# Two row fetches on two queues, a bias table behind one of them, six fills for eight and a new order: an attention and expert kernel

## The chip, the cores and the metric

The kernel runs on one core of a Trainium2 chip. The metric is device microseconds of one execution, the median of three runs. Engines are named as the profile names them: PE (TensorE matmuls), PEld (its weight loads), DVE (VectorE), ACT (ScalarE), POOL (GpSimd), SP (SyncE, which issues most DMAs). SPq and ACTq are the instruction streams of SP and ACT where they issue a DMA.

## What is computed

Eight batches, eight heads, 576 positions, head size 64, all float32. First, attention with a causal window of 128 positions and a bias that falls with distance; its result x is then read by four experts, each a full causal attention with its own projections, mixed by the two best of four gate values.

```python
scores = scale * np.matmul(q, k.transpose(0, 1, 3, 2))
bias = slopes[:, None, None] * (-np.abs(rel))[None, :, :]
mask = (rel >= 0) & (rel < window)
scores = np.where(mask, scores + bias[None], -1000000000.0)
attn = np.exp(scores - scores.max(-1)); attn /= attn.sum(-1) + 1e-09
x = np.matmul(attn, v)                      # heads side by side: (8, 576, 512)
logits = x @ w_gate                         # the best 2 of 4 experts, softmax over the two
for e in range(E):
    q, k, v = x @ wq[e], x @ wk[e], x @ wv[e]
    a = softmax(scale * q @ k.T, causal)
    out += weight_of(e) * (a @ v @ wo[e])
```

## The kernel before

Two heads are handled together as a "pair"; there are 32 pairs g, four to a batch. A pair's scores are taken in blocks of 128 rows; each block is added to a bias table and reduced to its row maximum by one DVE instruction (CUSTOM_DVE_ANT_0, called ISA in the program's order), raised by ACT, scaled by POOL or ACT, transposed on PE, and multiplied with v on PE. PSUM holds eight 128x512 tiles (ps0 to ps7).

The first batch's pairs are started in two halves so that work can begin on little data. For the first half, `fetch(g, 1, 0)` brings the rows of the first two blocks of pair g with two DMAs, one for each head (64 partitions of 2x256 floats, 128 KB). All eight go to tiles w100 (pairs 0 and 1) and w101 (pairs 2 and 3). `half_s` and `first_blocks` make the products, and use the table FT (it lies in the tile KKm) that DVE and POOL make out of the bias table tbt, which comes by a DMA of 160 KB. idt is the identity for the transposes. Then the projection weights are loaded: `wload(c)` brings one chunk of 386 KB (in_wall; there are four), `wprep(c)` rounds it to its high part WH (on POOL or ACT) and takes the low part WL (on DVE or POOL). The projections of x multiply chunk by chunk: the tile wx0 of x goes with the first chunk, wx3 with the fourth.

Ahead of all PE work stand "fills" (`warm`, lines 396 to 400): products of a zeroed tile AHTm, 128x512, which nobody reads.

The order of the work is not that in which the code stands. All instructions are recorded into a list (`_Rec`), and `plan` (line 201) puts them out in the order of the table ORDER, which also picks, where `nc.any` gave two choices, the engine. A negative place in ORDER is a fill:

```python
d = lo + 256 * hi
at += (d >> 1) ^ -(d & 1)
if at < 0:
    out.append(alt["fill"])
    continue
i = nodes[at // 2]
out.append(alt.get(i, [ops[i]])[at % 2])
```

Since one place issues everything, nearly every row of the trace has line 1229; rows are told apart by tiles and times. The change touches `fetch` (line 347), the three lines at the head of the emission (`zero()`, the table, the identity) and ORDER.

Of the kernel before, what the change touches and what calls it, by code (L numbers as in the profile page):

```python
# [19 lines left out]
B, H, S, D = 8, 8, 576, 64  # L20
DM = H * D
E = 4
P = 128
# [20 lines left out]
    "b3juEI|B5+l{K*2T#ZFbxq3n=;IMtT1a~MMI_4YiV8m{UccbBmBvWv#s!d9)?n)2tO!(<Xr&i>sj5MF2L(7KhM4D!Hq&5aY0TREpagutw@WEF^80x0A}N_"
    "AIHdMnGX{dei8<A6ll0RKi1?}n@TiOVuipfA+q^!e|Ifi85qxtt084$MOhgpYkrZXYck(5cio-Q3T`u)TGQ|OX5}1<vpV~d<tR&Hh+{B6r@13Pt!q=s&q>"
    "QGEHPJ(52Y8om+eXfvzy2$AN(f3(Jg>e*tT03SnP6m3mrRN3CUYnj$c*^vyw8&f^GP6G9;zy%NfS)7cx?m59=iOmE;_V8qalrvvjzvH7+^)Lb#=<xF9X-$"
    "v1xTwQv6=Y(!g4&LKKn3NeXU*)db<2<9bH;MkO{1ZOnGn!fwe^>00uw6V3i2a(p8Ew;K-qTWXFue1W+%2w;D>tF}A>tP9?ep`4v14edwQ$S%8V5N?|)yj1"
    "5l{CEbzkUhy1~C(xRVHO6ul};=Q&M8X#bMGVg@0o)S!rl)fbSGP*1w9kF3rQj<%P?kJPL7+JXb+N?cmb&@I%8%oLQaTYKKE}R@XtwrEVE9?xZH?gne)$k|"
    "nUJa=>*})<AU}VFR|=wA3;6k^A0n#SmVEe&~+aKiE$mXr=qt*lgMJ-)^<orv_uEXgIJ{#Td*Vhd+5P*#UL!p4K+Zfu|ZGrwD6>iI@MjcMzZ=5fYMz24R4V"
    "Fu85!x&dHpsWf$cYeUPzLWX-5Qrs{L1~?rntDe0$O8}-m@BZanZJqD|8WzbSq7y#)I_n7jP_Jx#;d`u$5qB2`ALuB^vyVJZl6wFF*!#2ZGc0H@(RiD3?W("  # L50
    "iSjvRs15ZUh8*xKF;V@1|lR&EKUE$u6d9X(C}-1ZDaCC0I>>dIv6+T=#0;$oMsghgK8q3hxKG%qAJAvz>6-)YOaxwsPHN!y|}m|3cXh=t4D<@UU}13$D^7"
    "OTpuFp`y<m+yIY`d81Ug(JSOE(>6!wmRHY;IcjO&EqMU9u9?iXn>`(abA6nIO&z4KYXiNQsDX8*rn@|2wAQ7OT-Io1urkJ!EEPMSckWM0PWBL?H=d^=(x}"
    "UVcoy>&<D4wE4*WL(`&;}%rP=0AMe86o39gj&0AI4-NUBxdiCW!8l0XtjsF+J=iVk3<(QG98^kK}7`6}g4T7oJO~_HF*`xHd6p~H|=~lK=TEE%)%IcD`(K"
    "8fpYP5G*yE-m7X;dN|*nvHT?gH$vZPFZ{kUU}CX;hk6trL_5tg0!}d%@FawjJ+!h8VGWdPdu+_kz^+Ww*i_EzXhNitapsd|XZrWJ69mq-CZhTT_;uGw~%h"
    "mvg3jLnaJblxEVRm{Rbz)cIO`Z-o0Q-ZwSAytWKIw;UTgZ@*zTSr@#YqO$3!NB?7FjwmL@M8TOdFx_JrY-%WnK|-$o<ICY$F7H2lwDy)-hNrkX+r(xPWbU"
    "w4H8e}PPrl+L%dkZg=*<g?`>W#2yvO*k;tG26TA4|vAIc#=Vwp%@cyBB$z&x)v4l{tnwdDjXgR4l7gl#}n<j!+Ht63jWm`!1_oIqr&$xck;m*y@i!^)Tp7"
    "Pg*c6!WA<hk+`{t(TX8S_;})TQXx%kJ>>gtAsKKSs5frg{C@I4kc6$sY1d@YU0_iw1z~+#8)#GpGe0`;*wWx!eJlZf(QS4`T;fpYs!)1s*5S?ZqLn*J}N2"
    "6IN7R-8fG!9yOnz4_5ltu#}7&zp%8-4xFZkBbGjzm;B@c{e~yyYUl~P5BcRsMhsf=S^Ca~TJ@-t(K-Rsa^>J{){&?4Z2Evl-0zfYRAU%oitP<aLTJz#B4D"
    "+~5jy?YO8tTG|>=t`t&HUVAoN~Mo@<$)}(Sv36=_xEVA=$+4eJEjo(oLd}%Idnt8oEYkh+=oVMHatHl4i(*zk1>cbBLYiY@dDl&w+M#hK>xkySrEmbauCP"
    "beTPafMhyA6IedU%I?l>Z96{9>+Hr5MCMs(qo=j#u(GArvDOW!yj*=CF%DB0<@<KjT4Apq9;;9;Py_PBAat6B`vw_n_b`()v#MGXRTP%8YbG#v%X63J)Sn"  # L60
    "u?(GNa$l{S3oq0X|JAGiGisw$3G8yalR%ZZ<5zkzqi+v!nPe$JlA&8j2UxH6)Z$Z@lYI%G8rT^Z_ajw=V6-ObT416LO<@d-DS<!Si-bGG+CWM9gxrAh}`o"
    "vCk$U3J}pa;L2=LY=mG|K#Rw{k=~p^-X=#v+VV^jv^N?Nv}z+;H66pX!1acwPxf>U&A7V-2B+HiI+MSyC4c#^%6t^M2#Tg?sNU8!rEFhsiIW^5JqBw?<xt"
    "|R6gdjNH3N5s?nLd0BsS&(#NXfy}KY+5v3R!*OculIyY8qw!QIbj|D<)2Ah?!)5K*V*h{J$R)}r<%x_oQLUU#(sw-xjNgFg~+RK#56H*T#Gq*zJTSxUB%`"
    "@}kX1EAV<-?B9?aAbr9>raobR$y(O+_hWC|j$Ubu1#b0*%iQ@~FGh3A3|!v2UJTfyFsA2_<@V5U8hUkk&g-03DIzFhu&%bo1Ku2Y*uj@ROep2I<j<<*y?@"
    "_Kt%41gZ1*u=B)##l+<UED&eO86cq_{9-Bm7x@{a?jDD(^zF7B9^@1rS{3{7K>v)rwZawA#4=KEA$czJ`erRdYd8ku#WV1#_t_Of9FZ(a&QnU6Y(8?7S^x"
    "RvRk{WnYvxM1<HGmfwJARjdmuaO*3^sleCNN5Z$j04UvFP8$w`E3FrK<=_VnxkWE`gMZKs(cl@w-<mg5qmAn)VvbgqRZOTP)#LW5vZxYD7@x$;v<T&9^Uc"
    "x~e^-_w5CvbA0XVOJO|Uh%>lc(3sLm#yG#3~!(lgHUg=4|+RFEt6i8HQW(ylI4{#*jgiGevMP&)zv2CSC{ky*ba>kiz>54KnP0g&B80M2FraYmD$}TSAPr"
    "ShbL*tJW5*z(h)#gM*g7E<LMbk$Hi<`TF`OQ9qM&vubkGnGC*EANuFL^wpL7zymK$q)^!y(efr&@QQ=Ko++|!{DD+-DaEw-r(?JVgt>HuxGdliR+|T{&N7"
    "-M+y`k(cuRZ^APZe|^UQch(7=TCqqTLx}rdb)h4e<GgL9`1{bkbjrmTEZ;EeqW2T8_bN4Iwe2wK;-<RcLK~@Nd5GFa0C0eQteod2ODeP^~7Wk?BIY1d1#2"
    "Wz%<!i>dvDDTrwK?LW@SFPa#dBxGzC8c5_UWYZQ_S!b(d)}~5_r_nvR%uE(#CrR#|j%l%U4ik0?<BezoilO?R2dp4-+dHC=&pt(yhels|tbEYbJ-!~hI-Z"  # L70
    "@*(%95OZDLpNB+OmHyQX1kW{Q=bbfCd+cK`6#d8uixN8B&{bw*Ywss8q0DKSS<TL&Eqr`B}bAV3Q$@80$v)Iss*pWH(ybO1MaEUf9I`Wmo;<Ba17Xh6keg"
# [1245 lines left out]
```

## Time and profile before

| what | value |
|---|---|
| median of three runs | 462.22 us (461.86 to 462.54) |
| the profiled execution, its own time | 461.31 us |
| its span | 459.5 us |
| PE busy | 452.8 us, 99% |
| PEld busy | 400.3 us, 87% |
| DVE busy | 386.3 us, 84% |
| ACT busy | 367.6 us, 80% |
| POOL busy | 246.8 us, 54% |
| share of PE in the chain that ended last | 87% |

Busy shares are averages over the whole span. Matmuls are pipelined, so that their records overlap: a busy PE can still have short holes. The page's forty slices show PE at nine tenths in all but the first and the last. What the change touches by name lies in the first 25 us; the order is other everywhere.

### The profile page before, as it was taken

The page shows a single profiled execution, that of the slowest core. Times are in us where ns is not written, and L with a number is a line of the kernel's source. Part 1 is how long each engine was busy: PE and PEld are TensorE (multiplying, and loading weights), DVE is VectorE, ACT ScalarE, POOL GpSimd, SP SyncE. Part 2 cuts the span into 40 slices and gives each one's busy share as a digit, 9 for nine tenths or more (in the row PEclk, how much of TensorE's full clock was granted, in tenths as well). Part 3 has the DMA queues.
Part 4 walks back from the last instruction along what each step waited for, and adds up shares of the span by engine and source line. Part 5 has one row for each costly group of instructions (what it writes and reads, how often), then busy time and mean ns, then how long its engine had stood idle before and what let it go on. Part 6 is the DMA issues. An engine that isn't in the chain of part 4 may idle for free.

```text
span 459.5 us, 18916 instructions
## 1 busy us (share of the span) xinstructions
PE 452.8 (99%) x7100; PEld 400.3 (87%) x7100; DVE 386.3 (84%) x1801; ACT 367.6 (80%) x1393; POOL 246.8 (54%) x498
## 2 busy tenths in 40 slices
...
GB/s 191 271 213 156 219 115 61 33 62 132 88 3 208 9 66 99 85 208 28 97 162 81 3 120 190 88 4 10 140 193 104 58 4 3 150 3 1 3 116 116
DMA packets 28252, 44.76 MB, mean 97 GB/s; under 512 B 7680, under 2 KB 14208, under 8 KB 28160
## 3 DMA queue, kind: packets, MB, share of 16 engines
...
q8 instruction: 56, 0.92, 0.8%
...
q14 instruction: 36, 0.29, 0.2%
...
## 4 chain that ended last, share of the span: by engine, by line
PE 87%; DVE 5%; ACT 2%; DMA 2%; POOL 2%; issue 1%; SPq 0%; POOLq 0%; ACTq 0%; DVEq 0%
PE ps L1229 87%; DVE w L1229 2%; ACT w L1229 2%; POOL w L1229 1%; DMA w<-in_rd 1%; DVE ps L1229 1%; DMA w<-in_wall 1%; DVE WL L1229 1%; DVE MPL L1229 0%; ACT MPL L1229 0%; DVE r L1229 0%; POOL MPL L1229 0%; DVE wx L1229 0%; DVE mr L1229 0%; POOL wx L1229 0%
## 5 line engine op out<-in xcount | busy, mean ns | idle before, releaser
L1229 ACT COPY w<-ps 128x512 f32<-128x512 f32 (+4 forms) x252 | 99.5, 445 | 33.7 <-PE ps L1229 29.2
L1229 ACT ACTIVATE w<-w,nm 128x128 f32<-128x128 f32 x252 | 98.7, 395 | 13.0 <-DVE nm L1229 12.7
L1229 PE MATMUL ps<-wx,WH 128*128 128x288 f32 (+2 forms) x512 | 107.5, 299 | 0.0
L1229 POOL TENSOR_SCALAR w<-w,mr,w 128x128 f32<-128x128 f32 (+3 forms) x128 | 79.8, 635 | 29.4 <-DVE mr L1229 16.7
L1229 POOL TENSOR_SCALAR w<-w,r 128x128 f32<-128x128 f32 (+1 forms) x163 | 60.9, 387 | 52.6 <-DVE r L1229 14.8
L1229 PEld LDWEIGHTS ps<-wx,WH 128*128 128x128 f32 x512 | 82.0, 189 | 2.4 <-DVE mnm L1229 0.7
L1229 ACT ACTIVATE w<-w,mnm 128x512 f32<-128x512 f32 (+3 forms) x128 | 71.2, 561 | 5.2 <-DVE mnm L1229 4.9
L1229 DVE TENSOR_TENSOR w<-ps,tmt 128x768 f32<-128x768 f32 (+2 forms) x92 | 69.8, 775 | 5.4 <-PE ps L1229 5.0
L1229 DVE CUSTOM_DVE_ANT_0 w<-ps,tbt 128x128 f32<-128x128 f32 x272 | 68.7, 284 | 0.9 <-PE ps L1229 0.2
L1229 PE MATMUL ps<-wx,WL 128*128 128x288 f32 (+2 forms) x256 | 68.5, 296 | 0.0
L1229 PE MATMUL ps<-w 64*64 64x128 f32 (+4 forms) x1200 | 63.5, 309 | 0.1
L1229 PE MATMUL ps<-WH,wx 128*128 128x260 f32 x288 | 61.4, 288 | 0.9 <-ACT WH L1229 0.9
L1229 PE MATMUL ps<-w,vt 64*64 64x192 f32 (+4 forms) x1344 | 59.7, 282 | 0.0
L1229 PE MATMUL ps<-idt,w 64*128 64x64 f32 (+1 forms) x1160 | 58.4, 230 | 1.0 <-POOL w L1229 0.9
L1229 PEld LDWEIGHTS ps<-w 64*64 64x64 f32 (+1 forms) x1200 | 50.2, 135 | 8.4 <-issue 1.4
L1229 PEld LDWEIGHTS ps<-w,vt 64*64 64x64 f32 (+1 forms) x1344 | 52.4, 133 | 5.2 <-issue 1.9
L1229 PEld LDWEIGHTS ps<-idt,w 64*128 64x128 f32 (+1 forms) x1160 | 47.7, 139 | 7.8 <-issue 2.0
L1229 DVE COPY_PREDICATED ps<-mkt,ps 128x64 f32<-128x64 int32 (+2 forms) x184 | 53.3, 313 | 1.2 <-PE ps L1229 0.5
L1229 PE MATMUL ps<-w,w 64*64 64x64 f32 (+7 forms) x1088 | 52.5, 307 | 0.0
L1229 DVE COPY w<-ps 128x256 f32<-128x256 f32 (+5 forms) x94 | 42.4, 469 | 11.8 <-PE ps L1229 11.1
L1229 PE MATMUL ps<-KKm 64*64 64x288 f32 (+8 forms) x640 | 50.5, 410 | 0.0
L1229 ACT ACTIVATE w<-w,r 128x128 f32<-128x128 f32 (+1 forms) x125 | 45.0, 398 | 6.2 <-DVE r L1229 3.9
...
## 6 DMA issues: line engine op xcount, KB each, us to landing
...
w<-in_hd SPq DMA_DIRECT2D x14, 128.0 KB, 3.3
w<-in_wall SPq DMA_DIRECT2D x4, 386.0 KB, 5.5
out<-w SPq DMA_DIRECT2D x8, 128.0 KB, 2.4
...
```

The lines of the kernel that those rows point to most:

```text
L1229: getattr(getattr(tc.nc, e), m)(*a, **k)
```

## The change

The two row fetches of pairs 0 and 1 get a choice of queue (SP or ACT), and so do the bias table and the identity. ORDER is replaced: the new one has six negative places for eight, puts one fetch of pair 0 on ACT ahead of the table, the identity on SP, and has another order of all engines. The recorded steps are the same; with the new table 309 of the steps that have a choice go to the other engine, and in the sums over the program PE differs by the two fills alone.

```diff
 ORDER = (
-    "c-pOae^g{=dH>w|K6Bp}?lm)JrkRN|DOgCM2U;-j6)IFPpb!TO2`DsRAVP%}6bx9fV8AfCRA`t82^=AX1PoMAsE{sZX@}!(52Rq>8!)Vabg|HYUHr0^HDF"
+    "c-p0S4NxT4b#C{)XZl{YTRSb!NHg(_i?N0n9B{yf5=bC{1!YiX95w<8Vvr$*XYhjr9FP|op4k_0AO;5%P(WfLa6pDKM6hBdu)%@^94N6aD1ieun=A?I>?Y"
...
@@ -344,7 +344,11 @@
             for j in range(2):
                 o = D * j * row + (QW + S + 2 * P) * j
                 src = bass.AP(tensor=a.tensor, offset=a.offset + o, ap=[[row, D], [QW - P * j, 2], [1, n]])
-                nc.sync.dma_start(v2[D * j : D * j + D, z, :, :n], src)
+                row_fetch = (v2[D * j : D * j + D, z, :, :n], src)
+                if g < 2:
+                    nc.any(*[(e, "dma_start", row_fetch, {}) for e in ("sync", "scalar")])
+                else:
+                    nc.sync.dma_start(*row_fetch)
             return
...
     zero()
-    nc.scalar.dma_start(tbt[:, 3], tb[:, 3])
+    nc.any(*[(e, "dma_start", (tbt[:, 3], tb[:, 3]), {}) for e in ("scalar", "sync")])
     for g in range(4):
         fetch(g, 1, 0)
-    nc.scalar.dma_start(idt, ident)
+    nc.any(*[(e, "dma_start", (idt, ident), {}) for e in ("scalar", "sync")])
```

What the table does is seen in the order of each engine. First place: the heads of the queues of SP and ACT. Before, SP:

```order
L1229 DMA w100_91<-in_hd 64x2x256 x4
L1229 DMA w101_92<-in_hd 64x2x256 x4
L1229 DMA w100_91<-in_rd 128x2x320
L1229 DMA w100_91<-in_hd 64x2x256 x2
L1229 DMA vt0_125<-in_vd 128x256
```

and ACT:

```order
L1229 DMA tbt_107<-in_tb 128x640
L1229 DMA idt_105<-in_ident 128x128
L1229 ACT_TABLE_LOAD
L1229 ACTIVATE w50_82,sm0_115<-w50_82,nmA0_129 128x128 x2
L1229 ACTIVATE w50_82,sm0_115<-w50_82,nmA0_129 128x256 x2
```

With the change, SP:

```order
L1233 DMA w100_91<-in_hd 64x2x256 x3
L1233 DMA idt_105<-in_ident 128x128
L1233 DMA w101_92<-in_hd 64x2x256 x4
L1233 DMA w100_91<-in_hd 64x2x256
L1233 DMA w100_91<-in_rd 128x2x320
L1233 DMA w100_91<-in_hd 64x2x256
```

and ACT:

```order
L1233 DMA w100_91<-in_hd 64x2x256
L1233 DMA tbt_107<-in_tb 128x640
L1233 ACT_TABLE_LOAD
L1233 ACTIVATE w50_82,sm0_115<-w50_82,nmA0_129 128x256
L1233 ACTIVATE w50_82,sm0_115<-w50_82,nmA0_129 128x128 x2
```

One of the four fetches into w100 went to the head of ACT, the table stands behind it, and the identity stands fourth on SP. Further down SP's queue the four weight chunks stand behind 16, 22, 25 and 27 DMAs, where before it was 14, 17, 20 and 24.

Second place: PE around the first products with the fourth weight chunk (those that read wx3). Before:

```order
L1229 MATMUL ps1_70<-WH_111,wx1_78 128x260 x2
L1229 MATMUL ps1_70<-WH_111,wx2_79 128x260 x2
L1229 MATMUL ps1_70<-WH_111,wx3_80 128x260 x2
L1229 MATMUL ps1_70<-WL_112,wx0_77 128x260
L1229 MATMUL ps1_70<-WL_112,wx1_78 128x260
L1229 MATMUL ps4_73<-wx3_80,WH_111 128x256 x2
L1229 MATMUL ps7_76<-w101_92 128x192
```

With the change:

```order
L1233 MATMUL ps7_76<-wx1_78,WH_111 128x256
L1233 MATMUL ps6_75<-WH_111,wx1_78 128x260
L1233 MATMUL ps7_76<-wx1_78,WH_111 128x256
L1233 MATMUL ps3_72<-wx1_78,WH_111 128x256
L1233 MATMUL ps3_72<-wx3_80,WH_111 128x256
L1233 MATMUL ps5_74<-idt_105,w54_86 128x128
L1233 MATMUL ps3_72<-wx3_80,WH_111 128x256
```

Ahead of the first wx3 product stand 24 products of the other three chunks' high parts before and 30 with the change, and the two 128x192 products of w101, which stood behind it before.

Third place: DVE in the softmax blocks of pairs 5 (nm5) and 6 (nm6); the TENSOR_TENSOR rows with tmt split transposed blocks of pair 4. Before:

```order
L1229 ISA w50_82,nm5_155<-ps6_75,tbt_107 128x128
L1229 ISA nm5_155 128x1
L1229 COPY_PREDICATED ps7_76<-mkt_106,ps7_76 128x128
L1229 TENSOR_TENSOR wx3_80<-ps2_71,wx3_80 128x256
L1229 ISA w51_83,nm6_161<-ps7_76,tbt_107 128x128
L1229 ISA nm6_161 128x1
L1229 ISA w51_83,nm6_161<-ps7_76,tbt_107 128x128
L1229 ISA nm6_161 128x1
L1229 TENSOR_TENSOR w102_93<-ps3_72,tmt_108 128x6x2x64
```

With the change:

```order
L1233 TENSOR_TENSOR w100_91<-ps4_73,tmt_108 128x6x2x64
L1233 ISA w50_82,nm6_161<-ps7_76,tbt_107 128x128
L1233 ISA nm6_161 128x1
L1233 COPY lg0_143<-ps0_69 128x4
L1233 TENSOR_TENSOR w100_91<-ps3_72,tmt_108 128x6x2x64
L1233 ISA w56_88,nm5_155<-ps5_74,tbt_107 128x128
L1233 ISA nm5_155 128x1
```

Two splits of 128x768 (6x2x64) of pair 4 now stand ahead of the last two blocks of pair 5; before, the first of them came behind pair 5's last block.

## Rows read from the trace of the kernel before

**Rows 1.** The page: heading and first section.

```profile
span 459.5 us, 18916 instructions
PE 452.8 (99%) x7100; PEld 400.3 (87%) x7100; DVE 386.3 (84%) x1801; ACT 367.6 (80%) x1393; POOL 246.8 (54%) x498
```

**Rows 2.** Busy time by stretch: engines, PEclk, DMA share, GB/s.

```profile
2.00:4.00 2.00, 2.00 (x6) 1.52 (x6) 0.93 (x2) 0.92 (x1) 0.85 (x2) 1.00 0.93 247
10.00:15.00 5.00, 4.74 (x59) 3.35 (x57) 4.93 (x28) 4.91 (x21) 3.28 (x10) 1.00 0.94 269
15.00:20.00 5.00, 5.00 (x47) 4.12 (x46) 4.97 (x26) 4.49 (x20) 3.79 (x9) 1.00 1.03 281
20.00:25.00 5.00, 4.08 (x50) 3.37 (x49) 4.93 (x17) 2.90 (x13) 4.19 (x6) 1.00 1.07 246
25.00:30.00 5.00, 5.00 (x42) 4.90 (x41) 4.96 (x26) 5.00 (x24) 3.55 (x7) 1.00 0.87 192
40.00:60.00 20.00, 20.00 (x338) 18.30 (x331) 19.41 (x113) 17.30 (x80) 8.45 (x23) 1.00 0.70 175
```

**Rows 3.** Waits of PEld, whole span: us, times, longest.

```profile
PEld ps L1229 <- ACT w L1229: 4.9, 18, 0.5
PEld ps L1229 <- DVE w L1229: 2.8, 10, 0.5
```

**Rows 4.** The timeline's first 7 us: start, us, engine, tiles, idle before.

```profile
0.74 5.34 SPq L1229 DMA_DIRECT2D w<-in_hd  x8
1.10 3.78 PE L1229 MATMUL ps<-AHTm 128*128 128x512 f32 x8 [1.10 <-POOL AHTm L1229]
3.03 0.29 DVE L1229 TENSOR_SCALAR KKm<-tbt 128x256 f32<-128x256 bf16 x1 [3.03 <-DMA tbt<-in_tb]
3.36 0.82 DVE L1229 TENSOR_TENSOR KKm<-KKm,tbt 128x256 f32<-128x256 f32 x1
4.13 0.40 DVE L1229 TENSOR_SCALAR mkt<-tbt 128x128 int32<-128x128 bf16 x1
4.81 4.42 PE L1229 MATMUL ps<-w 64*64 64x128 f32 x64
5.80 0.29 DVE L1229 CUSTOM_DVE_ANT_0 w<-ps,KKm 128x128 f32<-128x128 f32 x1 [1.23 <-PE ps L1229]
6.40 0.29 DVE L1229 CUSTOM_DVE_ANT_0 w<-ps,KKm 128x128 f32<-128x128 f32 x1 [0.30 <-PE ps L1229]
6.62 0.42 DVE L1229 CUSTOM_DVE_ANT_0 w<-ps,KKm 128x256 f32<-128x256 f32 x1
6.96 0.42 DVE L1229 CUSTOM_DVE_ANT_0 w<-ps,KKm 128x256 f32<-128x256 f32 x1
```

**Rows 5.** DMA issues by stretch: KB each, us to landing; first 1.2 us, then 14.3:17.

```profile
tbt<-in_tb ACTq DMA_DIRECT2D x1, 160.0 KB, 2.3
w<-in_hd SPq DMA_DIRECT2D x1, 128.0 KB, 3.4
idt<-in_ident ACTq DMA_DIRECT2D x1, 64.0 KB, 3.2
...
w<-in_wall SPq DMA_DIRECT2D x1, 386.0 KB, 6.9
```

**Rows 6.** The timeline around the projection weights, 14 to 25 us.

```profile
14.99 0.82 PE L1229 MATMUL ps<-w 128*128 128x192 f32 x4
15.49 1.35 SPq L1229 DMA_DIRECT2D w<-in_wall  x1
18.83 1.82 PE L1229 MATMUL ps<-wx,WH 128*128 128x256 f32 x14
22.88 0.74 PE L1229 MATMUL ps<-WH,wx 128*128 128x260 f32 x4
24.10 0.91 ACT L1229 CAST WH<-w 128x260 fp32r<-128x260 f32 x2
24.54 0.51 PE L1229 MATMUL ps<-WH,wx 128*128 128x260 f32 x2 [0.92 <-ACT WH L1229]
```

**Rows 7.** DVE groups by shape, 35 to 60 us.

```profile
L1229 DVE TENSOR_TENSOR w<-ps,tmt 128x768 f32<-128x768 f32 x4 | 3.8, 944 | 0.0
```

**Rows 8.** PE groups by shape: 4.9 to 6.1 us, then 6.6 to 9.2 us.

```profile
L1229 PE MATMUL ps<-w 64*64 64x256 f32 x4 | 1.1, 631 | 0.0
...
L1229 PE MATMUL ps<-w 64*64 64x256 f32 x28 | 2.4, 387 | 0.0
```

More of the change, by code (lines that the diff above doesn't have):

```diff
@@ L44 @@
[L44 to L71, printed above, removed]
@@ new lines @@
+    "4D!Vq^+ep*h9RT12>5C^&ItX*UW3UC|((gpY<@8#jzw>L0L$Sh6GnAMu(YXL4wur{~S;dk1JK29ClTX46eQW3cuIB<Flaz*i4&*fmQ{lVc`JUsePZhR6U&"
+    "BaK-!dB?)>AW5>tNZwT@P!pS_ktp8(_A!be&*K!CnARSCiJ-z744~6+nijt?Y)aWSQcnh7RZi&ul!-waqNA0c1fcNz6DnR$}%*dOO7dH>PHj3KDzcQ&Mk6"
+    "gPlzkP63kAz0oJ_3W2astd^(d__QV5-BK+Ijskwg3S^{ZzcD2|s;lF_ztY#-(w<#`U6X^kFbKH>%%#dc&c@U_yik}2#aWP@T{`YdzmRt&z87o&ElD^c@*}"
+    "F{_2i7AqqL=sQqq+|m7=t9Y$rrksluknk=^+gS5HQXleTtEoD8|VeCF0BpwXinsT~&p%>2z=hMGI<{~>=`iSLiORG+0}V_yPf|KguEr{J*{$g_X^l|PJ&W"
@@ new lines @@
+    "-T{X0V0T+lV4KVld!r!Ww*$+m1&i@6Pmmi5~<JAPpPbeY<5Kv`E(5mYRo4)t2fH|*iEef)R9*R1;zcJR=yEWwq4#6mqWpJW?3j*tp=!B%X{VZOYkuXSF~f"
+    "T&pgbrKkZuGfSNvL+?JN+%q?~I7PQ@}5q|Wrl~|}sFsa5R0BWIXQwuCWv2~xe!)tFe!O#A6Yci>>2BO@_x1RdK*3RWWj~gGEzgb%~cze5liI3c?fJIR)sz"
+    "P#=oZ%YldSViQJE|CppqPC<ctnQH3U4V7^$&gXnbhHKyG8m`+7t}n-Wlm!{S5_Ec~`dn`76|^w6!+bTn-AOSr9%DS<_kTfGgq9fs>jjJo25_!!jV!LFEg0"
+    "5vqoCG{8-OiiE)t4X9g_a0NV2u?4VQnY9kE3`<u5!^+xJdBuD0Os_uwiGJMPH`LZidaRw&n{C;BmO}wLd+Y=!n3eEfeIz0>A=PP(PJlPV6!I#Hap652TUn"
@@ new lines @@
+    "KBi;jb&cr{7}$LzSnnxk%ev%S4g18`-wDX)}dZ){(ys`RqOQ2T_%yI!r3zC$^6zm$d_rKS<j`o6M9ylS3hdf-oAqeA+PJ~MGy-gq<pG$qyva$NY9r!epQ?"
+    "?w&GE%HrOR7<b<B4heGV3S^g&NgU=arS!TZ_KokG0n>)e;3#JY|f-%!wPi4p7$ls)5#f7p}&w&Hyg#h1)JAkTWiq3#(-&Nq4}Bl8fK^2$Y1{AHl`H+@N2a"
+    "kypzo^l@J4vn+?z=eG4++1QzHbkf|%9GO?3+>8G-jm>IqKWP+{KLYbW*kKD#X9mn{jeDkh_%2t~~t)yq5Z-7AqM=Uj6ss{^ml{%P0%=OJz_dJb+Y~&Tnu?"
+    "}lWY+_v%&`Qe)zLtL5TXk}PZ*MAO>*a6c)RWG{6mS!@xOa1741fPmq^G3E8#Cr;)iI$;IW?#BE7VM;2SN5Z``i16>dc<~;!H>R4FDFa+2CUw&bXs5H(6!O"
@@ new lines @@
+    "e%@54WHM@joZ@sACw1WPe)6S_g2sVeH+EUDRetn$NpJt|2#KZrYd{!z$xxbJmg#NWSHmxOhTnd&oiQ8qcCm0DjNdu^QA#F#0f_4)zoA9_=HCMgg~i<n0Gp"
+    "-o`Cs<HNHkH%&K$wfDmEvK=Y9XYd{tQ*`bkg5e~_=7UzX*WEBTGkxGXyXuCm~SwG|e`;lNCuZntoE;<#wI8?&{(g_ZhzPcD#tk|kSZ)zWO9V>_}INT#Hty"
+    "<?jy6Gge1g(tA`H|S_cY0I2%Y__gOWG6$*Vj^QSr*jFaE2=A|W~XMW*V|IZNYRu+^82d~EzSdX8uKxOmB%&%DKSNiLwY$2N6j`<^U9_AYi$)1qv>hsv@)K"
+    "(_kHk8h8&ymP0zdX{#?u<{`uoY_SE^Av~Vh$uTZSa$&j{o5fb9c`^pQts}?Rll2X13<&0Wdp`|?`wyks7x(QuS&M;X~4cE1Oeh0-4L^eY3n%-nY39$LxM;"
```

102 lines of the change are left out of this document (57 added, 45 removed).

## The prediction

> **What bounds the kernel now.** The page comes first: PE is busy 99% of the span [rows 1], so that outside its edges only a shorter stream of PE work, or holes too short for that figure, can be worth much. The table of stretches comes second, because the 99% is a mean over stages. There the reader sees the start: in 20 to 25 us PE has 4.08 us of 5, and from 10 us to 60 us DVE is full (4.93 to 4.97 of each 5 us, 19.41 of 20) [rows 2]. The DMA share is 0.93 to 1.07 in those early stretches. So the first 25 us hang on three things at once: DVE's queue, the bytes that must come, and PE's order. The timeline is read third, to see what DVE waited for at its start [rows 4], and around the projection weights, where PE's one long hole stands, 0.92 us before 24.54, released by ACT's rounding of the fourth weight chunk [rows 6]. After 25 us PE is never shown idle for long; a lead that PE has there is a lead at the end, if the body's order is no worse.
>
> The sum is made against the profiled execution: 461.31 us, 1.8 us more than its span. That is 0.9 us under the median of the three runs, 462.22; a difference worked out here is put on the median. Under 0.2%, about 0.92 us, one can't tell this kernel's change from none.
>
> **The change, part by part.**
>
> *Six fills for eight.* Eight take 3.78 us from 1.10, so 0.47 each [rows 4]; six end at 1.10 + 6 x 0.47 = 3.9. They come to nothing by themselves, either way: what covers them is PE's wait for the rows. The first fetch needs 3.4 us from its issue at 0.74 [rows 4, 5], so it lands at 4.1. If the rows came before 3.9, two fills fewer would be worth up to 0.9 us.
>
> *The second row fetch on ACT.* Eight fetches take SP 5.34 us, 0.67 each [rows 4]. On SP the second is issued 0.67 us behind the first and lands at 1.41 + 3.4 = 4.8, which is where the first products start. At the head of ACT both land at about 4.1, and PE can begin 0.7 us earlier. SP saves one fetch (0.67) and gets the identity; the transposes need that only when a block has been scaled, 5 us later, and its landing takes 3.2 us [rows 5], so it costs them nothing.
>
> *The table behind it.* Here the gain is paid back in part. The table was issued at 0.74 and landed 2.3 us later [rows 5]; DVE began on it at 3.03 and had the bias ready at 3.36 + 0.82 = 4.2, long before PE's products, for which it waited 1.23 us [rows 4]. Now its issue waits for ACT's fetch, to 0.74 + 0.67 = 1.41. Lower end: 1.41 + 2.3 = 3.7. Upper end: what followed the table on that queue, the identity, took 3.2 us, so 4.6. In 2 to 4 us the DMA engines are 0.93 busy at 247 GB/s [rows 2], so the 128 KB that now stand ahead cost 0.5 us of transfer: 3.7 + 0.5 = 4.2, which I take. Behind it DVE does the conversion (3.03 to 3.36, 0.33), then the mask (0.40), which the new order puts ahead of the addition, then the addition (0.82) [rows 4]: ready at 4.2 + 1.55 = 5.75, between 5.25 and 6.15.
>
> The Trainium skill ("DMA: Bandwidth & Descriptors", section "Issuing engines are not separate DMA queues") says that DMAs started from different engines run on the same DMA engines and interleave, and that starting them in parallel saves only the issue time. If each queue brought its own bandwidth, the lower end would stand, and the start would gain 0.9 us; by the rule it is nearer the upper end, and the start gains little. The trace shows two queues at work at 0.93 of the engines, which agrees.
>
> What was the start worth before? Four blocks of pair 0 are done at 6.96 + 0.34 = 7.30. Back to back they take 2 x 0.22 + 2 x 0.34 = 1.12 (6.40 to 6.62, 6.62 to 6.96) [rows 4], so DVE stood as if it had begun at 6.18. With the bias at 5.75 it begins 0.43 us earlier, at the ends 0.9 or 0.0. DVE waits now for the table, no longer for PE; POOL, which makes the other pairs' tables from the same bias, starts later than it did, and its scaling of pair 0 gains less. I carry 0.3 us to PE at 24 us.
>
> *PE's order around the fourth weight chunk.* Six more products with the other chunks stand ahead of the first with wx3, and two of 128x192. At 1.82 / 14 = 0.13 and 0.82 / 4 = 0.2 us each [rows 6] that is 0.78 + 0.4 = 1.2 us of work put into a hole of 0.92 us. PE came to the hole at 22.88 + 0.74 = 23.6; now it comes at 23.6 - 0.3 + 1.2 = 24.5. Is the chunk there? It was issued at 15.49 and landed 6.9 us later, 22.4 [rows 5, 6]. It now stands behind 27 DMAs on SP for 24. By place: (15.49 - 0.74) / 24 = 0.61 each, issue at 17.2, landing at 24.1. By bytes, since the engines are full: ahead of it are 128 KB of pair 2 and 3's tail and 32 KB of small ones more, 160 KB at 269 GB/s (10 to 15 us) [rows 2], 0.6 us, so 23.0. The rounding takes POOL about what ACT needed for both parts, 0.91 [rows 6], the first part some 0.6: ready at 23.6 by bytes, 25.0 by place for both parts. I take the bytes, because the DMA share stays near 1. Then PE has no hole; at 24.5 it stands 1.2 us further than it did at 24.54. By place it would be 0.7.
>
> The later second and third chunks (22 and 25 DMAs ahead for 17 and 20) are covered by w101's 64x192 products, which now stand ahead of all weight products. If that cover fails, PE waits there and the 1.2 us shrinks towards 0.4.
>
> *The rest of the order.* PE's work is the same but for the fills. Its waits are drawn anew: those of PEld on ACT and DVE are 4.9 + 2.8 us in 28 [rows 3], 0.28 each. If each changes by its own size, the sum moves by 0.28 x the root of 28, 1.5 us, with no sign. The tail ends in the same steps. I set it at nothing and give it to the range.
>
> Sum: 0.3 + 0.9, **1.2 us less**: 460.1 for the profiled execution, 461.0 for the median.
>
> **The rivals.**
>
> *Nothing is left at the end (462.0).* DVE is full up to 60 us [rows 2]. If DVE, and not PE's hole, limits this stage, only its earlier start counts, 0.43 us less, and PE's lead at 24.5 is spent waiting for blocks; with the table at its upper end not even that. For it: DVE's 4.9 of 5. Against it: PE is shown busy in 25 to 30 us, 5.00 of 5, so that it had other work.
>
> *Slower (463.7): DVE's queue at pair 5.* Two splits of 128x768 for pair 4 now stand ahead of pair 5's last two blocks. Each takes 0.94 us [rows 7], so the blocks come 1.89 us later at about 46 us, and behind them wait ACT's exponents, their scaling and PE's transposes of pair 5. In that stretch DVE has 0.6 us free of 20 [rows 2] and can't make it up. 1.89 less 0.43 is 1.46 slower: 462.22 + 1.46 = 463.7. It decides if PE has less than 1.9 us of other work in its queue ahead of pair 5's transposes. Against it: the splits have to be done anyway, and pair 4's products come sooner.
>
> *TensorE's lower clock lasts longer (462.4).* Products of 64x256 take 631 ns before 6.1 us and 387 ns after 6.6 [rows 8]; fills come every 0.47 us. The first is the 1.2 GHz level, the second 2.4, although the granted clock reads 1.00 throughout. Now PE stops between the fills' end, 3.9, and 4.1, or longer if the rows are late, and the rise may come later. If it came after 9.2 us, the products of 6.6 to 9.2, 2.4 us of busy time, would take up to 1.3 us more, of which DVE's own pace hides a part; all of it takes the 1.2 us away. The Trainium skill ("TensorE: Matmul & The Clock Gate", Part 1) says that the clock starts low, that activity releases it, and that idle time brings the low state back, out of step with the kernel's start; no run yet shows a gap's effect here.
>
> That the change does not do what it says is excluded by the order shown above.
>
> **How the numbers follow.** My forecast 0.46; nothing left 0.28; slower by DVE's queue 0.20; the clock 0.06, two thirds of it inside 0.2%. So faster by over 0.2% has 0.46, within 0.2% 0.32, slower 0.22. The time is the likeliest case's, 461.0; its own range is 459.5 to 462.3, by 1.5 us of redrawn waits. For 8 in 10 the range goes from 459.0, two us under the forecast (1.5 us and the table at its lower end), to 463.6, nearly the slower rival's time.
>
> **What would show it.** Right: the first CUSTOM_DVE row near 5.75, waiting on the table or on DVE's own addition, not on PE; the first 64-row product near 4.1; no PE wait on WH near 24 us; PE busy in 20 to 25 us above 4.08. Wrong in the table: DVE's first conversion after 4.6. Wrong in the weights: PE idle with a release by POOL's or ACT's WH, or by in_wall. Wrong in the body: the start is as said, and the lead at 25 us is gone by 60 us with PEld waits on DVE between, or later in another place.

## The result, and the profile after

The changed kernel takes **466.24 us** (466.12 to 466.57, 4 runs) against 462.04 for the kernel before (461.17 to 462.54, 4 runs): a ratio of 1.0094, interval 1.0077 to 1.0112. By that ratio it is 4.3 us slower (4.2 by the medians); the prediction, 461.0 (459.0 to 463.6), had the wrong sign. The two profiled executions, one of each kernel, differ by 4.8 us in their spans, 464.3 against 459.5 [rows 1].

The page of the changed kernel: heading, first section, and the shares of the chain that ended last.

```profile
span 464.3 us, 18919 instructions
...
PE 453.6 (98%) x7098; PEld 400.2 (86%) x7098; DVE 389.0 (84%) x1806; ACT 366.1 (79%) x1392; POOL 243.6 (52%) x494
...
PE 74%; DVE 13%; POOL 7%; ACT 3%; issue 2%; DMA 1%; POOLq 0%; DVEq 0%; ACTq 0%
```

The chain's line of the kernel before:

```profile
PE 87%; DVE 5%; ACT 2%; DMA 2%; POOL 2%; issue 1%; SPq 0%; POOLq 0%; ACTq 0%; DVEq 0%
```

PE's idle time has grown from 6.7 us (459.5 less 452.8 [rows 1]) to 10.7 (464.3 less 453.6): four of these 4.8 us. In the chain PE's share was 87%; it is 74%, and DVE and POOL have 20% where they had 7%. So PE waits more often for these two. The stretches say where it begins (columns as in [rows 2]):

```profile
2.00:4.00 2.00, 2.00 (x5) 1.01 (x4) 0.00 (x0) 1.28 (x1) 0.00 (x0) 1.00 0.81 222
10.00:15.00 5.00, 3.95 (x56) 2.60 (x49) 4.81 (x31) 5.00 (x23) 4.08 (x10) 1.00 0.88 243
20.00:25.00 5.00, 5.00 (x62) 4.43 (x59) 4.85 (x23) 5.00 (x24) 4.59 (x9) 1.00 0.96 238
25.00:30.00 5.00, 3.69 (x31) 3.48 (x31) 4.72 (x22) 2.69 (x12) 2.95 (x6) 1.00 0.58 171
40.00:60.00 20.00, 20.00 (x306) 18.78 (x306) 19.48 (x109) 18.09 (x84) 6.93 (x23) 1.00 0.88 210
```

DVE, which worked 0.93 us in 2 to 4 us, does nothing there now. PE's hole of 20 to 25 us is gone, as predicted (5.00 for 4.08), and one of 1.3 us stands in 25 to 30, where PE had been full. In 10 to 15 us PE has 3.95 for 4.74; from 40 to 60 us it is full in both. The timeline of the first 9 us, to set beside [rows 4]:

```profile
1.10 2.93 PE L1233 MATMUL ps<-AHTm 128*128 128x512 f32 x6 [1.10 <-POOL AHTm L1233]
1.50 0.61 ACTq L1233 DMA_DIRECT2D tbt<-in_tb  x1
...
4.60 1.55 PE L1233 MATMUL ps<-w 64*64 64x256 f32 x12 [0.58 <-DMA w<-in_hd]
5.04 0.29 DVE L1233 TENSOR_SCALAR KKm<-tbt 128x256 f32<-128x256 bf16 x1 [4.07 <-DMA tbt<-in_tb]
...
5.59 0.41 DVE L1233 TENSOR_TENSOR KKm<-KKm,tbt 128x256 f32<-128x256 f32 x1
...
6.18 0.42 DVE L1233 CUSTOM_DVE_ANT_0 w<-ps,KKm 128x256 f32<-128x256 f32 x1 [0.18 <-PE ps L1233]
...
6.67 3.26 PE L1233 MATMUL ps<-w 64*64 64x128 f32 x38 [0.52 <-DVE nmA L1233]
...
8.80 0.29 DVE L1233 CUSTOM_DVE_ANT_0 w<-ps,KKm 128x128 f32<-128x128 f32 x1 [1.09 <-PE ps L1233]
```

The first products start at 4.60, 0.2 us earlier than before (4.81); the table is there at 5.04, 2.0 later (3.03); the first block is reduced at 6.18 instead of 5.80. The landings behind it, by the view of DMA issues of the first 8 us (KB each, us to landing), with [rows 5]:

```profile
tbt<-in_tb ACTq DMA_DIRECT2D x1, 160.0 KB, 3.5
w<-in_hd ACTq DMA_DIRECT2D x1, 128.0 KB, 3.0
```

From its later issue the table needs 3.5 us, where it needed 2.3. From 6.7 us on PE's pace is the second loss of the start in this execution. PE's groups by shape in 8 to 9 us (busy us, mean ns):

```profile
L1233 PE MATMUL ps<-w 64*64 64x256 f32 x12 | 1.9, 631 | 0.0
```

Before, these products took 387 ns from 6.6 us on [rows 8]; now they take 631 up to 10 us. That is the 1.2 GHz level for some four microseconds more, though the granted clock reads 1.00 throughout.

PE's new hole, and what DVE and POOL do ahead of it (timeline, 25 to 28 us, engine by engine):

```profile
27.84 0.33 PE L1233 MATMUL ps<-idt,w 128*128 128x128 f32 x1 [1.31 <-DVE nmB L1233]
...
25.55 1.35 DVE L1233 TENSOR_TENSOR WL<-w,WH 128x260 fp32r<-128x260 f32 x1
26.82 0.42 DVE L1233 COPY_PREDICATED ps<-mkt,ps 128x256 f32<-128x256 int32 x1
27.27 0.29 DVE L1233 CUSTOM_DVE_ANT_0 w<-ps,tbt 128x128 f32<-128x128 f32 x1
...
27.49 0.29 DVE L1233 CUSTOM_DVE_ANT_0 w<-ps,tbt 128x128 f32<-128x128 f32 x1
...
28.44 0.42 DVE L1233 TENSOR_TENSOR WL<-w,WH 128x260 fp32r<-128x260 f32 x1
...
25.32 1.29 POOL L1233 TENSOR_TENSOR WL<-w,WH 128x512 fp32r<-128x512 f32 x1
```

A transpose waits for a PSUM tile that the second of the two blocks at 27.27 and 27.49 sets free. Ahead of both stands a split WL of 260 columns. It takes 1.35 us while POOL runs a split of its own (25.32 to 26.61), and the same shape takes 0.42 at 28.44, where no POOL instruction is running when it begins (the next one begins at 28.67).

Last, PEld's waits over the whole span (us, times, longest), with [rows 3]:

```profile
PEld ps L1233 <- POOL w L1233: 6.3, 15, 0.9
PEld ps L1233 <- ACT w L1233: 4.8, 17, 0.5
PEld ps L1233 <- DVE w L1233: 2.7, 8, 0.4
```

The waits on ACT and DVE are what they were (4.9 in 18, 2.8 in 10). Those on POOL were 2.4 us in 6, by the same view of the kernel before:

```profile
PEld ps L1229 <- POOL w L1229: 2.4, 6, 0.9
```

The longest lie far behind the places that the prediction speaks of (timeline, POOL and PE at 129 to 133 us, PE at 362 and 397 us):

```profile
129.68 2.19 POOL L1233 TENSOR_SCALAR w<-w,mr,w 128x512 f32<-128x512 f32 x3
131.85 0.36 POOL L1233 TENSOR_SCALAR w<-w,r 128x128 f32<-128x128 f32 x1
...
132.27 1.95 PE L1233 MATMUL ps<-idt,w 64*128 64x64 f32 x51 [0.65 <-POOL w L1233]
...
362.05 1.16 PE L1233 MATMUL ps<-idt,w 64*128 64x64 f32 x30 [0.46 <-POOL w L1233]
...
397.09 1.09 PE L1233 MATMUL ps<-idt,w 64*128 64x64 f32 x28 [0.78 <-POOL w L1233]
```

The first: the scaling of one block of pair 12 at 131.85 is what PE's transposes wait for. Its inputs were ready at 125.2; ahead of it POOL has eight rescalings of expert blocks (w<-w,mr,w). With the order before, the scalings that PE waits for in these places and at 190.8 us (a weight load's wait of 0.27) were done 3.5 to 9 us ahead of PE's use, two of the four by ACT.

How late PE is, at equal work: in each profiled execution PE's products after the fills are summed in order by their columns, and the times compared at which the same sum is reached. The columns give the lag behind the kernel before, in us; e3 to e13 are experiments below.

| before's time | changed | e3 | e4 | e5 | e12 | e13 |
|---|---|---|---|---|---|---|
| 20 | 1.0 | 0.9 | 1.2 | 1.2 | 0.1 | 1.7 |
| 35 | 1.6 | 1.4 | 1.1 | 1.8 | 0.6 | 1.2 |
| 130 | 0.4 | 2.0 | -0.2 | 1.2 | 0.2 | 0.0 |
| 140 | 1.3 | 2.0 | 0.7 | 2.3 | 1.1 | 0.9 |
| 200 | 2.5 | 2.0 | 1.5 | 3.2 | 2.4 | 1.9 |
| 310 | 2.6 | 2.3 | 1.9 | 3.0 | 2.3 | 1.9 |
| 400 | 4.6 | 2.7 | 3.9 | 3.9 | 2.9 | 2.5 |
| end | 4.8 | 2.6 | 3.8 | 3.8 | 2.9 | 2.8 |

The changed kernel is late by 1.6 us at 35, catches up to 0.4 at 130, and then loses 4.4 in steps: at 132, 140 to 200, 319, 362 and 397 us. These are single executions, and the table is for places, not for prices: e4 and e13 have the start of before to 36 us, and in their profiles PE is 1.2 and 1.7 us late at 20 all the same, since both waited there for the landing of vt (1.06 and 1.53 us).

### The profile page after: what moved, and what is told of

Read it like the earlier page. It is cut to its first block, busy times and chain, and to the rows that moved or that the text cites. A ratio compares the mean times of both kernels' runs of the same rounds, so it can differ in the third digit from the quotient of the medians.

```text
span 464.3 us, 18919 instructions
## 1 busy us (share of the span) xinstructions
PE 453.6 (98%) x7098; PEld 400.2 (86%) x7098; DVE 389.0 (84%) x1806; ACT 366.1 (79%) x1392; POOL 243.6 (52%) x494
## 4 chain that ended last, share of the span: by engine, by line
PE 74%; DVE 13%; POOL 7%; ACT 3%; issue 2%; DMA 1%; POOLq 0%; DVEq 0%; ACTq 0%
PE ps L1233 74%; DVE w L1233 7%; POOL w L1233 6%; DVE ps L1233 3%; ACT w L1233 2%; DMA w<-in_hd 1%; DVE wx L1233 1%; DVE r L1233 0%; ACT MPL L1233 0%; DVE mr L1233 0%; DVE MPL L1233 0%; POOL MPL L1233 0%; DVE WL L1233 0%; DVE nm L1233 0%; POOL AHm L1233 0%
## 5 line engine op out<-in xcount | busy, mean ns | idle before, releaser
L1233 ACT COPY w<-ps 128x512 f32<-128x512 f32 (+4 forms) x242 | 96.3, 452 | 43.1 <-PE ps L1233 32.8
L1233 POOL TENSOR_SCALAR w<-w,mr,w 128x128 f32<-128x128 f32 (+3 forms) x128 | 82.7, 657 | 40.3 <-DVE mr L1233 38.3
L1233 ACT ACTIVATE w<-w,mnm 128x256 f32<-128x256 f32 (+3 forms) x128 | 71.1, 559 | 4.8 <-DVE mnm L1233 3.1
L1233 PE MATMUL ps<-idt,w 64*128 64x64 f32 (+1 forms) x1160 | 59.6, 230 | 4.9 <-POOL w L1233 3.1
L1233 PE MATMUL ps<-w,vt 64*64 64x192 f32 (+4 forms) x1344 | 62.0, 283 | 0.1
L1233 PE MATMUL ps<-WH,wx 128*128 128x260 f32 x288 | 60.3, 289 | 0.0
L1233 DVE COPY w<-ps 128x256 f32<-128x256 f32 (+5 forms) x104 | 45.9, 462 | 12.1 <-PE ps L1233 11.1
L1233 PE MATMUL ps<-w,w 64*64 64x64 f32 (+7 forms) x1088 | 53.9, 306 | 0.0
L1233 PE MATMUL ps<-KKm 64*64 64x288 f32 (+8 forms) x640 | 49.3, 410 | 0.0
```

Source lines behind the costliest of these rows:

```text
L1233: getattr(getattr(tc.nc, e), m)(*a, **k)
```

## The experiments

The theory to be tested first: the head costs 1 to 2 us and the rest of the order the remainder. The rival: it is all carried from the head. All kernels are built on the changed code by another list of places in ORDER; all were timed in five rounds against the kernel before, which alone ranged from 460.6 to 464.7 us in them; so the intervals are 1.2 to 2.8 us wide. "+" is the ratio less one, times 462 us, with its interval.

**e1 and e2, the heads exchanged.** e1 is the order before with the change's head, e2 the change with the head of before (all eight fills). The edit of e1 on PE and ACT (on SP the identity takes the place of the fetch that went to ACT):

```diff
 PE
-MATMUL ps<-AHTm 128x512 x8
+MATMUL ps<-AHTm 128x512 x6
 ACT
+DMA w100<-in_hd 64x2x256
 DMA tbt<-in_tb 128x640
-DMA idt<-in_ident 128x128
```

> The order of before, with the change's head alone: six fills, one row fetch of pair 0 on ACT ahead of the table, the identity fourth on SP. Theory 1 (the late table starts DVE and POOL about 1.5 us later, and the end pays it): 1.0 to 2.0 us slower than before, first TENSOR_SCALAR of DVE near 5.0 us. Theory 2 (the start is caught up in the first 60 us, the new order of the rest costs everything): within 0.9 us of before, with the same late first TENSOR_SCALAR.

> The order of the change, with the head of before: eight fills, table and identity on ACT, all row fetches on SP. Theory 1, if the rest only carries the late start: 462 to 463, the time of before. Theory 2 (the order of the rest costs by itself): 465 to 466.5. If both add: 464.5 to 465.2, 1.0 to 1.7 us under the change.

Measured: e1 462.25, 0.9998 [0.9983, 1.0013], so -0.1 us; e2 466.14, 1.008 [1.0049, 1.011], +3.7. **In the order before, the head is not the loss** (by e1's interval 0.6 us at most); within the change e2's interval leaves up to 2 us open. The head is late all the same: in e1 DVE begins on the table at 4.88, and PE lags by 1.3 us at 20 us. From 26 us it is 0.5. What gave it back is seen in the view of the tile WL, 15 to 30 us (ns min/median/max, starts). Before:

```profile
L1229 POOL TENSOR_TENSOR WL<-w,WH x5: 743/1292/1723, 19.5 to 26.7; 128x512 fp32r<-128x512 f32 x3, 128x260 fp32r<-128x260 f32 x2
L1229 DVE TENSOR_TENSOR WL<-w,WH x3: 389/1417/1499, 20.0 to 23.0; 128x260 fp32r<-128x260 f32 x2, 128x512 fp32r<-128x512 f32 x1
```

e1:

```profile
L1232 POOL TENSOR_TENSOR WL<-w,WH x5: 741/1290/1302, 19.6 to 27.1; 128x512 fp32r<-128x512 f32 x3, 128x260 fp32r<-128x260 f32 x2
L1232 DVE TENSOR_TENSOR WL<-w,WH x3: 390/618/1408, 21.3 to 23.5; 128x260 fp32r<-128x260 f32 x2, 128x512 fp32r<-128x512 f32 x1
```

The 260-column split that took 1.50 us on DVE takes 0.62, since DVE, being late, no longer begins it behind POOL's second split of 512 columns but behind a rounding of 0.85 us: 0.9 us of the 1.3. The rows are in the last section.

**e3 and e4, start and body exchanged.** The first 455 places reach to about 36 us. e3 has them from the change and the rest in the order of before; e4 the other way round.

```diff
-ORDER = before[:455] + before[455:]
+ORDER = change[:455] + before[455:]
...
-ORDER = change[:455] + change[455:]
+ORDER = before[:455] + change[455:]
```

> The change's order for the first 455 places (to about 36 us, its head among them), then the order of before. The trace of the change is 1.6 us behind before at 32 us and 4.8 at the end. If the two stretches add: before plus 1.2 to 1.8 us, 463.2 to 463.9. If the order of the rest is what absorbs or enlarges a late start: as before (462) or above 464.5.

> The order of before for the first 455 places (to about 36 us, its head among them), then the order of the change. If the two stretches add: before plus 2.8 to 3.5 us, 464.8 to 465.5. If the later waits of the change only follow from its late start: 462 to 462.9.

Measured: e3 463.7, 1.0026 [1.0009, 1.0043], +1.2 (0.4 to 2.0); e4 465.39, 1.0068 [1.0041, 1.0095], +3.1 (1.9 to 4.4). The two add up to the whole, 4.3. **Most of the loss lies behind 36 us**, and it is there even when the start is the old one.

**e5, four scalings earlier on POOL.** In the change, four of POOL's instructions that PE waited for (two scalings of attention blocks, two rescalings of expert blocks) are put ahead of work that nobody waits for yet. One of the four:

```diff
 TENSOR_SCALAR w53_85<-w53_85,r12_5_223 128x128
+TENSOR_SCALAR w53_85<-w53_85,r12_0_220 128x128
 TENSOR_SCALAR w58_90<-w58_90,mr1_0_0_221,w1_199 128x384
...
 TENSOR_SCALAR w50_82<-w50_82,mr1_0_1_222,w1_199 128x128
-TENSOR_SCALAR w53_85<-w53_85,r12_0_220 128x128
 COPY mr1_1_2_227<-w1_199 64x1 x2
```

> The change, with four scalings on POOL moved ahead of 1 to 8 others that stood in front of them in POOL's queue, nothing else. In the trace of the change PE waits 0.82, 0.33, 0.66 and 0.97 us for them (132, 191, 362 and 397 us), while their own inputs were ready 3 to 16 us earlier. Theory (POOL's queue, not the amount of work, is what the new order lost in the body): 2.0 to 2.8 us under the change, 463.4 to 464.3. Rival (POOL is full there, so that the wait only moves to the next thing that PE needs): within 0.9 us of the change.

Measured: 464.63, 1.0052 [1.0034, 1.0069], +2.4 (1.6 to 3.2), where the change has +4.3 (3.6 to 5.2). The intervals are apart: **1.9 us come back for four instructions moved in one queue**, just short of the 2.0 to 2.8 expected. (The rows above give 0.65, 0.46 and 0.78 us for PE's idle time at 132, 362 and 397 us, less than the waits in the expectation.) PEld's waits on POOL are nearly what they were before; in the timeline the waits at 191 and 397 us are gone, the other two went to the next thing in line:

```profile
133.54 0.67 PE L1231 MATMUL ps<-idt,w 64*128 64x64 f32 x14 [0.84 <-DVE wx L1231]
...
362.05 1.15 PE L1231 MATMUL ps<-idt,w 64*128 64x64 f32 x30 [0.38 <-POOL w L1231]
```

```profile
PEld ps L1231 <- POOL w L1231: 2.7, 8, 0.6
```

**e6 and e7, the hole at the fourth weight chunk.** e6 is the kernel before with ACT's two roundings of that chunk put ahead of two scalings; e7 is e6 with the change's head. They ask what the 0.92 us hole [rows 6] was worth, and whether it was the cover that hid the late head in e1.

```diff
-ACTIVATE w_90<-w_90,r_4_138 128x128
-ACTIVATE w_82<-w_82,r_4_140 128x128
 CAST WH<-w_89 128x260
 CAST WH<-w_89 128x512
+ACTIVATE w_90<-w_90,r_4_138 128x128
+ACTIVATE w_82<-w_82,r_4_140 128x128
```

> Before, with ACT's two roundings of the fourth weight chunk (WH) ahead of two scalings that stood in front of them on ACT; nothing else. In the trace of before PE waits 1.09 us for the first of them at 24.5 us. Theory (the chunk landed at about 22.4 us and the rounding stands behind scalings that wait for DVE): 0.6 to 1.1 us faster than before. Rival (the chunk itself is late, or DVE's full queue sets the pace after 25 us): within 0.4 us of before.

> The same as the run before it, with the change's head (six fills, a row fetch on ACT ahead of the table, the identity on SP). If the hole at 24.5 us was the cover under which the late start of the head cost nothing, then without it the head costs 0.7 to 1.3 us more than the run beside it. If something else covers it: the same time as the run beside it.

Measured: e6 462.47, 1.001 [0.9996, 1.0024]; e7 462.66, 1.0006 [0.9991, 1.0022]. Neither gains nor loses what can be told; e6 misses its theory (0.6 to 1.1 us faster) and comes out by its rival. In e7 PE's hole comes back 1.6 us later, behind a DVE block:

```profile
26.09 0.56 PE L1232 MATMUL ps<-w 128*128 128x192 f32 x2 [0.80 <-DVE nmB L1232]
```

So **closing the hole gained nothing that can be told** (by e6's interval 0.2 us at most). DVE sets the pace there: counted along each engine's own order, PE's lag behind the kernel before at 30 us is DVE's, 0.5 and 0.47 us in e1, 0.7 and 0.65 in e7, 0.4 and 0.38 in e9.

**e8, the new hole at 27.8 us closed** (e5, with DVE's two blocks ahead of the split):

```diff
-TENSOR_TENSOR WL<-w_89,WH 128x260
 COPY_PREDICATED ps_71<-mkt,ps_71 128x2x128
...
 ISA w_88,nmB_145<-ps_74,tbt 128x128
 ISA nmB_145 128x1
+TENSOR_TENSOR WL<-w_89,WH 128x260
 TENSOR_TENSOR WL<-w_90,WH 128x512
```

> The change with the four POOL scalings moved, and on DVE one mask copy and two softmax blocks of pair 3 moved ahead of the split of the second weight chunk's last 260 columns (1.35 us). In the trace of the change PE waits 1.49 us at 27.8 us for a PSUM tile that the second of these blocks frees. Theory: 3.0 to 4.2 us under the change, 462.0 to 463.2. Rival (the split is needed as soon as the tile is): no better than the kernel with POOL's four scalings alone.

Measured: 464.32, 1.0057 [1.0034, 1.008]. The transpose that started at 27.84 starts at 26.45 without a wait, and the time is that of e5. Nothing can be told of a gain, 1.7 us under the change where the theory was 3.0 to 4.2.

**e9 and e10, the fills alone.** e9 is the kernel before with six, e10 the change with eight.

```diff
-MATMUL ps<-AHTm 128x512 x8
+MATMUL ps<-AHTm 128x512 x6
```

> Before, with six fills for eight, nothing else. In the traces so far every kernel with eight fills has 64x256 products at 376 ns from about 6.4 us on, every kernel with the new head (six fills) has them at 631 ns until about 10.3 us. Theory 1 (the fills: with six PE stands idle from about 3.9 to 4.8 us and the rise to full clock comes 4 us later): 631 ns until about 10 us here too. Theory 2 (the late table, which makes PE wait in 5 to 9 us): 376 ns from about 6.4 us. Time by both: within 0.9 us of before, since DVE sets the pace to 60 us.

> The change, with eight fills for six, nothing else. By theory 1 of the run beside it: 64x256 products at 376 ns from about 6.5 us, by theory 2 at 631 ns until about 10 us. If the low clock of the first 10 us is what the change lost at its start: 1 to 1.5 us under the change. If not: within 0.9 us of the change, 465.4 to 467.1.

Measured: e9 462.35, 1.0002 [0.9986, 1.0019]; e10 465.11, 1.0065 [1.004, 1.009], +3.0 (1.8 to 4.2). With both row fetches on SP, as before, e9 shows when the rows are there (timeline, weight loads of PE from 3.5 us):

```profile
3.97 0.29 PEld L1232 LDWEIGHTS ps<-w 64*64 64x64 f32 x4 [0.67 <-DMA w<-in_hd]
4.62 0.30 PEld L1232 LDWEIGHTS ps<-w 64*64 64x64 f32 x8 [0.35 <-DMA w<-in_hd]
```

The first products can start at 3.97 and the next at 4.62: what held them to 4.81 in the kernel before was the eight fills, not the rows. (In the profiles of six other kernels with eight fills the start is at 4.80 or 4.81 too.) PE's groups in 8 to 9 us of e9, of e10, and of e12, which is described below and has six fills:

```profile
L1232 PE MATMUL ps<-w 64*64 64x256 f32 x8 | 1.5, 631 | 0.0
...
L1232 PE MATMUL ps<-w 64*64 64x256 f32 x15 | 1.3, 383 | 0.0
...
L1231 PE MATMUL ps<-w 64*64 64x256 f32 x12 | 1.2, 402 | 0.0
```

In all eight profiles with eight fills these products are at the 2.4 GHz level by 7 us, and in seven of the eight with six fills at the 1.2 GHz level until 9 us or later. But the eighth, e12's, has them at the higher level from 4.6 us on, with the same six fills. So the two fills go with an early rise, and do not decide it alone; what else does is not shown. In the order before they are worth nothing that can be told at the end. In the change they may be worth a microsecond; e10's interval overlaps with that of the change, so this stays open.

**e11, an attempt at a faster kernel before:** e6, and POOL's 512-column split behind its two of 260 columns, so that DVE's splits don't coincide with it.

```diff
-TENSOR_TENSOR WL<-w_88,WH 128x512
 TENSOR_SCALAR WH<-w_88 128x260
...
 TENSOR_TENSOR WL<-w_89,WH 128x260
+TENSOR_TENSOR WL<-w_88,WH 128x512
```

> Before, with ACT's two roundings of the fourth weight chunk ahead of two scalings (as in an earlier run) and, on POOL, the split of the third chunk's 512 columns moved behind the splits of 260. In before DVE's splits at 20 to 22.8 us took 1.42 us (512 columns) and 1.50 us (260 columns) while POOL did splits of its own; with the new head, where they lay 1.4 us later, the second took 0.62. Theory (splits on DVE and POOL at the same time slow each other, and DVE sets the pace there): DVE's second split 0.4 to 0.7 us here, 0.5 to 1.2 us faster than before. Rival (PE has enough other work, or POOL's late split is waited for at 28 us): within 0.4 us of before.

Measured: 461.84, 0.9991 [0.9975, 1.0006], which cannot be told from no change; 0.5 to 1.2 us had been the theory. DVE's splits got short, by the tile view:

```profile
L1232 DVE TENSOR_TENSOR WL<-w,WH x3: 387/621/1269, 20.2 to 22.3; 128x260 fp32r<-128x260 f32 x2, 128x512 fp32r<-128x512 f32 x1
```

DVE was 0.75 us ahead at 25 us and 0.5 at 29; PE waited for a landing (0.41 us before 24.95), its weight load for POOL (0.38 before 27.24), and by 46 us DVE's lead was gone.

**e12, e13 and e14, more of the same mending.** e12 is the change with e5's moves (the one at 362 us widened to three rescalings of that block), the DVE blocks of e8, and what the two remaining waits hung on, moved ahead too (a subtraction into wx, a reduction and its reciprocal on DVE, a rescaling of MPL on POOL). e13 has the start of before and e12's body; e14 the change's start with eight fills and e8's move, and the body of before. Two of e12's places:

```diff
+TENSOR_TENSOR wx2_79<-ps7_76,wx2_79 128x2x64
 TENSOR_REDUCE mr1_1_2_227<-msm1_118 128x1
 RECIPROCAL mr1_1_2_227<-mr1_1_2_227 128x1
-TENSOR_TENSOR wx2_79<-ps7_76,wx2_79 128x2x64
...
+TENSOR_SCALAR MPL0_120<-MPL0_120,mr5_0_2_378 128x576
 TENSOR_SCALAR w53_85<-w53_85,r28_0_372 128x128
 TENSOR_SCALAR w56_88<-w56_88,mr5_0_1_374,w5_353 128x512
-TENSOR_SCALAR MPL0_120<-MPL0_120,mr5_0_2_378 128x576
```

> The change with the places of the earlier kernel (three POOL scalings ahead, two blocks of pair 3 ahead on DVE), and the two waits to which its gain had moved: at 133.5 us one subtraction on DVE ahead of a reduction that waits for POOL; at 362 us POOL's rescalings of mp5_0_0 ahead of two others, and the rescaling of MPL0 earlier. Theory (the loss in the body is a sum of such single places): 0.7 to 1.6 us under the earlier kernel, about 463.0. Rival (POOL and DVE are late as a whole there, so that each place only uncovers the next): the same as the earlier kernel, 464.3.

> The order of before for the first 455 places, then the change's order with the POOL scalings and the DVE instructions moved as in the last kernel. With the change's body unmended it was 3.1 us over before. If the moved places are the body's whole loss: within 0.7 us of before, 461.8 to 462.9. If they are a part and the rest of the order loses too: 1.0 us or more over before.

> The change's order for the first 455 places, with eight fills and with the two blocks of pair 3 ahead of the split on DVE, then the order of before. With the start unmended it was 1.2 us over before. If the wait at 27.8 us and the late clock are the start's loss: within 0.5 us of before. If the start loses by its order as a whole (DVE stands still in 7 to 10 us): still 0.7 to 1.5 us over before.

Measured: e12 463.99, 1.0028 [1.0012, 1.0044], +1.3 (0.6 to 2.0); e13 463.81, 1.0044 [1.0025, 1.0062], +2.0 (1.2 to 2.9); e14 462.58, 1.0008 [0.9995, 1.002], +0.4, which cannot be told from before. So e12 has 3.0 of the 4.3 us back; that it is better than e5 or e8 cannot be told, since the intervals overlap. PE's longest wait on POOL in e12, and in e13:

```profile
132.63 1.57 PE L1231 MATMUL ps<-idt,w 64*128 64x64 f32 x43 [0.70 <-POOL mr L1231]
...
132.42 1.60 PE L1231 MATMUL ps<-idt,w 64*128 64x64 f32 x44 [0.69 <-POOL mr L1231]
```

At the same place the wait has its third object: the scaling, then DVE's subtraction into wx, now POOL's copy into mr. e13 came out by the second of its two branches (1.0 us or more over before): about 2.0 us of the body's loss are left with these places mended, and the gain over e4 is not clear of the noise. No version beats the kernel before.

## Why the prediction was wrong

- **"Six fills for eight", nothing either way.** Right for the end in the order before (e9). But with the new head the rows came at 4.3 to 4.6, not 4.1, and in seven of the eight profiles with six fills the lower level lasted some four microseconds longer. That is what the third rival said would happen. Its ground, that PE stops behind the fills, is not shown: e9 has products from 3.98 and no idle time of PE there by the profile, and was late; e12 stops for 0.30 us and was early. (Its 1.3 us are also 1.5 by its own rows, 2.4 x (631/387 - 1).) The price at the end is between nothing (e9) and about a microsecond (e10), unresolved.
- **"The second row fetch on ACT", 0.7 us earlier.** Wrong in its ground. I read the start at 4.81 as the second fetch's landing; it was the end of the fills. With SP alone and six fills the first rows are used at 3.97 and the next at 4.62 (e9). With one fetch on each queue the first products come at 4.60 here, and at 4.32 to 4.64 in the other profiles with this head and six fills: of the 0.7 us, 0.0 to 0.3 came.
- **"The table behind it", lands at 4.2, ready at 5.75, DVE 0.43 earlier.** Mis-sized with the wrong sign at DVE: 5.0, outside the range of 3.7 to 4.6, and the first block at 6.18, 0.38 later than before and released by PE, not by the table. I added 0.5 us of transfer; the fetch ahead and the later issue together cost 2.0 (in the other profiles with this head DVE begins at 4.70 to 4.92). That the bias was late by only 0.25 us, ready at 6.00, is luck: the addition took 0.41 us where I had read 0.82, because in the kernel before it had begun 0.27 us behind an instruction of POOL (last section). The Trainium skill ("DMA: Bandwidth & Descriptors", section "Issuing engines are not separate DMA queues") says that a second issuing engine saves the issue time alone. The traces agree: 0.67 us of issue was there to save, and no more than 0.3 came out of it. The 0.3 us carried to 24 us were a lag of 1.0 to 1.3.
- **"PE's order around the fourth weight chunk", 0.9 us won.** The step that I thought the gain. The chunk and its rounding came in time, and the hole went, as worked out. The gain did not come: PE met DVE's block at 27.8 us and stood 1.31 us. e6 and e7 show that even in the order before closing the hole brings no gain that can be told. The first rival (DVE, and not PE's hole, limits this stage) had the mechanism, and its row [rows 2], DVE 4.93 to 4.97 of 5 up to 30 us, was the one to believe. I had set PE's 5.00 of 5 against it; but that PE is busy in a stretch doesn't say that it will be when its work is moved up.
- **"The rest of the order", nothing, 1.5 us with no sign.** This is the step that failed: a term set at nothing, which measures 3.1 us (1.9 to 4.4, e4). I took the waits on ACT and DVE as the ones to be redrawn [rows 3]. They did come out the same. POOL's, which I had left out as few, went from 2.4 to 6.3 us. The order of POOL's queue, set beside the durations in the trace, could have shown it: the scaling of pair 12, which ACT had done by 127.2 for transposes that begin at 131.23, and there behind 6.3 us of other work (125.39 to 131.85), with inputs ready at 125.2. e5 shows 1.9 us of it by four moves. A remainder of 1.3 to 2.0 us (e12, e13) stays open. Part of it may be waits still: behind 36 us e13's profile has three of PE over 0.15 us, 0.69, 0.20 and 0.21, and before's has one, of 0.16.
- **The slower rival, DVE's queue at pair 5.** Its place came true and its price didn't. Counting the blocks along DVE's order, pair 5's last one is 4.1 us later than before, more than the 1.9 reckoned, and pair 7's 1.7. PE's lag is 1.8 us at 45, 1.5 at 55, 2.2 at 60 and 0.9 at 100: PE had other work, which was the condition that the rival named, and what the place cost at 60 us was given back.
- **The start as a whole** costs 1.2 us (0.4 to 2.0, e3), and 0.4 (-0.2 to 0.9) with eight fills and the DVE blocks ahead of the split (e14). The intervals overlap, so that these two do it is likely and not shown, and which of them isn't settled: e8 and e10 alone show nothing that can be told.
